# Mamba-2 scan and gated feed-forward on one core: the scan's visit for two pairs of sequences joined into one for all four, in chunks 2 to 5

## The chip, the core and the metric

The kernel runs on one core of a Trainium2 chip. Such a core has a matrix engine (TensorE, PE in the profile; its weight loads are PEld), an elementwise engine (VectorE, DVE), an activation engine (ScalarE, ACT), a general engine (GpSimd, POOL), and a queue for transfers (SyncE, SP). Each works through its own queue in order, and they wait for each other by semaphores. The metric is the device time of one execution in microseconds; lower is better.

## The reference

There are 4 sequences of 768 positions with 8 heads. Each head has a state of 16 by 32 (N by D). For chunks of positions, with L the product of the decays `a` between two positions:

```python
CB = np.einsum('bhin,bhjn->bhij', Cc, Bc)
y_intra = np.einsum('bhij,bhjd->bhid', CB * L, xc)
y_inter = np.einsum('bhin,bhnd->bhid', Cc, state) * decay_to_i[:, :, :, None]
y[:, :, sl] = y_intra + y_inter
Bx = np.einsum('bhjn,bhjd->bhjnd', Bc, xc) * decay_from_j[:, :, :, None, None]
state = decay_full[:, :, None, None] * state + np.sum(Bx, axis=2)
```

The heads' `y` side by side are the 256 columns of 3072 rows, which then go through a gated feed-forward layer in float32: `h = x @ w_in` (2048 columns), `g = h * cos(h)`, `out = g @ w_out`.

## The kernel before

**Chunks and steps.** The kernel takes chunks of 128 positions, so there are 6 of them, numbered 0 to 5, and in each all four sequences: 512 positions. The feed-forward part of one chunk is 16 steps, and a global step number `n` runs over all 96 (the loop at L739). `first(n)` makes one bank of `h` (hp, two banks in turn) by four matmuls with w_in; then ScalarE makes the whole turns `k`, VectorE the fraction `w` (L518), ScalarE the sine in place (L523, `gate`), and VectorE the product `gT` (L528, `gated`). Two steps later `second` multiplies it with w_out: from chunk 1 on by seven half-size products instead of eight (`seven`), for which GpSimd has to make differences `gd` of gT (L553 to L556) first. After steps 1 and 9 of a chunk's count, VectorE and ScalarE copy the finished banks to `ps`, GpSimd makes the output sums (L624), and SyncE stores them.

**The scan between the steps.** In chunks 1 to 5 the scan of one pair of sequences (`u` is 0 or 1; `b` is a sequence, two to a pair) is done in stages placed between the steps:

- `decays`: VectorE's running products `lam` (L344), two halves of four heads for each sequence, and GpSimd's scaled B, `sc`;
- `reaches` (L335): the running products of `a` along a chunk, one for each sequence;
- `turn2`: TensorE transposes B and C (tp), ScalarE copies them out as bT and cT, VectorE makes rT, which is C times the reach;
- `intra2`: TensorE's products C times B in two double banks, `g`;
- `masked`: VectorE's products `m` of g and lam, one sequence at a time;
- `finish2`, here called the visit: TensorE's products of the state (L447), then the products of m with x (L454), both into y; ScalarE copies y to yT, which is the input of the feed-forward part of that chunk; then the sums of the chunk (L471, `sum_up`), and `carry`, in which VectorE (`whole`) and GpSimd make the new state.

Two of the three products use only a strip of TensorE's 128 rows or columns, so four run beside each other: L447 on strips of 32 rows and 64 columns, L454 and L471 on 128 rows and 32 columns.

**The order.** The order of the queues is the order in which the program is written; no scheduler changes it. `TURN = (NF - 5, NF + 3)` with NF = 16 says at which step, counted from the start of the chunk before, a pair has its `turn2`: pair 0 at step 11, pair 1 at step 19, that is, step 3 of its own chunk. Its `intra2` is one step later, its `masked` one and two later, its visit three later, and its four half scans are at the four steps before it (chunk 1, pair 0, has its own places). So a visit comes every 8 steps, and half scans come one a step at most. In a step, VectorE's queue has w, rT if there is one, gT, the masked products, the carry, the half scan and then the reach scans. TensorE has first, the transposes, second, g and then the visit.

**Buffers.** tp, g, y and the sums take turns on two pairs of PSUM banks (`pair`), so y's bank is the first bank of g, and is free when masked has read it. `m` has two buffers in SBUF, rT, bT and cT one. `unit0`, `a0s` and `tos` are used at the start only and have memory of their own.

Of the kernel before, what the change touches and what calls it, by code (L numbers as in the profile page):

```python
# [8 lines left out]
FP32 = mybir.dt.float32  # L9
# [16 lines left out]
def kernel(  # L26
# [30 lines left out]
    V, ACT, G, PE = nc.vector, nc.scalar, nc.gpsimd, nc.tensor  # L57

    NB, H, S, D = x.shape
    N = B.shape[-1]  # L60
    P = 128
    NC = S // P
    DM, DF = moe_w_in.shape
    KT = DM // P
    NF = DF // P
    TB = NB * P
# [4 lines left out]
    W = P // 2  # L71

    const = ctx.enter_context(tc.tile_pool(name="const", bufs=1))
    loads = ctx.enter_context(tc.tile_pool(name="loads", bufs=3))
    rows = ctx.enter_context(tc.tile_pool(name="rows", bufs=NB))
    scan = ctx.enter_context(tc.tile_pool(name="scan", bufs=2))
# [3 lines left out]
    two = ctx.enter_context(tc.tile_pool(name="two", bufs=2))  # L80
# [8 lines left out]
    def pair(name):  # L89

        return psum.tile([P, 2, 4 * P], FP32, tag="scan", bufs=2, name=name)


    raw, arow, along = {}, {}, {}
# [124 lines left out]
    for b in range(NB):  # L219
# [4 lines left out]
        out=a_in, in_=a.rearrange("(u b) h (c p) -> (b h c) u p", u=NU, p=P))  # L224
# [9 lines left out]
    unit = const.tile([P, HH, P], FP32, name="unit")  # L234
    G.tensor_copy(out=unit, in_=ident.unsqueeze(1).to_broadcast([P, HH, P]))

    unit0 = const.tile([P, H, W], FP32, name="unit0")
    for t in range(2):
        ts = slice(t * W, (t + 1) * W)
        V.tensor_copy(out=unit0[ts], in_=ident[ts, ts].unsqueeze(1).to_broadcast([W, H, W]))  # L240
# [30 lines left out]
                    axis=mybir.AxisListType.XY, op=ALU.add)  # L271


    a0s = const.tile([P, 2, H, W], FP32, name="a0s")
    halves = a0z.rearrange("p (t i) -> p t i", t=2)
    for h in range(HH):
        ACT.activation(a0s[:, :, h], halves, AF.Copy, scale=mine[:, h:h + 1])
    for t in range(2):
        G.tensor_tensor(out=a0s[:, t, HH:H], in0=halves[:, t:t + 1].to_broadcast([P, HH, W]),
                        in1=mine[:, HH:H].unsqueeze(2).to_broadcast([P, HH, W]), op=ALU.mult)  # L280
    tos = const.tile([P, H, W], FP32, name="tos")
    G.tensor_tensor(out=tos, in0=to.unsqueeze(1).to_broadcast([P, H, W]),
                    in1=mine.unsqueeze(2).to_broadcast([P, H, W]), op=ALU.mult)

# [1 line left out]
    scaled, lam, reach, state, part, yT = {}, {}, {}, {}, {}, {}  # L286

    def heads(b):
        return slice(b * H, (b + 1) * H)
# [78 lines left out]
    def intra(b):  # L368
        bT, cT = part[0, b]
        g = [pair("g") for _ in range(2)]  # L370
        for q in range(4):
            r = slice(32 * q, 32 * q + 32)
            PE.matmul(g[q // 2][:, q % 2, 0:2 * P], lhsT=bT[r],
                      rhs=cT[r].rearrange("p t (s i) -> p s t i", s=2), start=True, stop=True)
        l = lam.pop((0, b))
        m = scan.tile([P, 2, H, W], FP32, tag="m", name="m")
        for q in range(2):
            of = [t[:, :, q * HH:(q + 1) * HH].rearrange("p s (k t) i -> p k s (t i)", k=2)
                  for t in (m, l)]
            V.tensor_tensor(out=of[0], in0=g[q][:, :, 0:2 * P].rearrange(  # L380
                "p k (s i) -> p k s i", s=2), in1=of[1], op=ALU.mult)
        part[0, b] = m
# [16 lines left out]
    def turn2(c, u):  # L399
        bc = raw[c][0]  # L400

        tp = pair("tp")[:, 0].rearrange("p (s k i) -> p s k i", s=2, k=2)
        for s in range(2):
            for k in range(2):
                PE.transpose(tp[:, s, k],  # L405
                             bc[:, k, heads(2 * u + s)].rearrange("p h n -> p (h n)"), ident)
        bT = scan.tile([P, 2, P], FP32, tag="bT2", bufs=1, name="bT2")
        ACT.copy(out=bT, in_=tp[:, :, 0])
        cT = scan.tile([P, 2, 2, P], FP32, tag="cT2", bufs=1, name="cT2")
        for t in range(2):  # L410
            ACT.activation(cT[:, :, t], tp[:, :, 1], AF.Copy, scale=slot[:, t:t + 1])
        rT = scan.tile([P, 2, P], FP32, tag="rT", bufs=1, name="rT")
        V.tensor_tensor(out=rT, in0=tp[:, :, 1], in1=reach[c, u], op=ALU.mult)
        part[c, u] = [bT, cT, rT]

# [10 lines left out]
    def masked(c, b):  # L426

        u, s = divmod(b, 2)
        g, ms = part[c, u][0:2]
        l = lam.pop((c, b))  # L430
        m = scan.tile([P, H, P], FP32, tag="m", name="m")
        for q in range(2):
            of = [t[:, q * HH:(q + 1) * HH].rearrange("p (k t) i -> p k (t i)", k=2)
                  for t in (m, l)]
            V.tensor_tensor(out=of[0], in0=g[q][:, :, s * 2 * P:(s + 1) * 2 * P], in1=of[1],  # L435
                            op=ALU.mult)
        ms.append(m)

    def finish2(c, u):
        (_, ms, rT), xr = part.pop((c, u)), raw[c][1]  # L440
        y = pair("y")


        for s in range(2):
            for q in range(4):
                r, p = slice(32 * q, 32 * q + 32), 64 * (q % 2)
                PE.matmul(y[p:p + 64, q // 2, s * P:(s + 1) * P],  # L447
                          lhsT=state[c - 1, u][r, s].rearrange("p t d -> p (t d)"),
                          rhs=rT[r, s], start=(s == 0), stop=False, tile_position=(32 * q, p),
                          skip_group_check=True)  # L450
        for s in range(2):
            for h in range(H):
                q, t = h % 4, h // 4
                PE.matmul(y[32 * q:32 * q + 32, t, s * P:(s + 1) * P], lhsT=xr[:, 2 * u + s, h],  # L454
                          rhs=ms[s][:, h], start=False, stop=True, tile_position=(0, 32 * q),
                          skip_group_check=True)
        if u == 0:
            yT[c] = two.tile([P, 2, TB], FP32, tag="yT", name="yT")
        ACT.copy(out=yT[c][:, :, 2 * u * P:(2 * u + 2) * P], in_=y[:, :, 0:2 * P])
        if c < NC - 1:  # L460
            s_ps = pair("s_ps")[:, 0, 0:4 * D].rearrange("p (s d) -> p s d", s=2)
            for s in range(2):
                sum_up(c, 2 * u + s, s_ps[:, s])
            carry(c, u, s_ps)

    def sum_up(c, b, s_ps):

        xr, sc = raw[c][1], scaled.pop((c, b))
        for q in range(4):
            two_ = slice(2 * q, 2 * q + 2)  # L470
            PE.matmul(s_ps[32 * q:32 * q + 32], lhsT=sc[:, two_].rearrange("p h n -> p (h n)"),  # L471
                      rhs=xr[:, b, two_].rearrange("p h d -> p (h d)"), start=True, stop=True,
                      tile_position=(0, 32 * q), skip_group_check=True)
# [47 lines left out]
    def gate(n):  # L521
        cos = turns[n]
        ACT.activation(cos, cos, AF.Sin, bias=quarter, scale=TWO_PI)  # L523
# [160 lines left out]
    for dst, src in ((a_cut, cut), (a_all, la)):  # L684
        nc.sync.dma_start(
            out=dst.rearrange("(u b) h (c p) -> (b h c) u p", u=NU, p=P), in_=src)
# [11 lines left out]
                 NF + 1: [(0, hind), (1, hind)], NF + 3: [(2, hind), (3, hind)]}  # L698


    TURN = (NF - 5, NF + 3)

    halves_of = {u: [(t - 4 + i, 2 * u + i // 2, i % 2) for i in range(4)]
                 for u, t in enumerate(TURN)}
    ahead = {1: {0: [(4, 0, 0), (6, 0, 1), (8, 1, 0), (9, 1, 1)]}}

    sums = {}

# [18 lines left out]

    def pairs(n):

        at = [(1 + (n - t) // NF, u) for u, t in enumerate(TURN) if (n - t) % NF == 0]  # L730
        return [(c, u) for c, u in at if 0 < c < NC]

    def halves_at(n):
        return [(c, b, t) for c in range(1, NC) for u in range(2)
                for m, b, t in ahead.get(c, {}).get(u, halves_of[u]) if m + (c - 1) * NF == n]

    EARLY = 3
    rest_of_loads()
    for n in range(NC * NF + LAG):  # L739
        c, f = divmod(n, NF)  # L740
        early = n < EARLY
        if n < NC * NF:
            if f == 0 and c > 0:
                load(c + 2)
            first(n)
            if n == 0:
                first_scan()
            for at in pairs(n):
                turn2(*at)
            rests = [grade(*piece[m], later=True)  # L750
                     for m in ((n,) if early else ()) + ((n + 1,) if n >= EARLY - 1 else ())
                     if m in piece]
            gate(n)
            for rest in rests:
                if rest:
                    rest()
            if not early and n in piece:
                join(*piece[n])
            gated(n)
            if early and n in piece:  # L760
                join(*piece[n])
            if n in (1, 2):
                carry(0, n - 1, sums[n - 1])
        for i, js in differ_at.get(n, ()):
            differ_w(i, js)
        if n >= LAG:
            second(n - LAG)
        for c, u in pairs(n - 1):
            intra2(c, u)
            masked(c, 2 * u)  # L770
        for c, u in pairs(n - 2):
            masked(c, 2 * u + 1)
        for c, u in pairs(n - 3):
            finish2(c, u)
            if u == 1:
                raw.pop(c)
        for c, b, t in halves_at(n):
            decays(c, b, t)
            if t == 1:
                load_a(c + 1, (b,))  # L780
        for c, u in pairs(n + 1):
            for b in (2 * u, 2 * u + 1):
                reaches(c, b)
                load_along(c + 1, (b,))
# [30 lines left out]
```

## Time and profile before

| | |
|---|---|
| time, median of 3 | 387.14 us (386.27 to 387.29) |
| profiled execution | 386.67 us, span 384.9 us |
| TensorE clock granted | 1.00 |
| L512, hp matmuls | 768, 184.4 us busy |
| L609, output products | 1106 in four forms, 274 to 277 ns each |
| L422 g, L454 y, L447 y, L471 sums | 160, 320, 160, 160 records |
| L344 lam | 40 scans, 1394 ns mean |
| L335 reach | 20 scans, 786 ns mean |
| L435 m | 40 products, 681 ns mean |

A float32 matmul stands as two records. The durations of matmuls overlap, as they are pipelined: what one costs is read from the distance between two starts (eight records of L512 take 1.73 us), not from its duration. Idle time of an engine is given with what ended it, in brackets.

### The profile page before, as it was taken

What the parts mean: (1) busy time and instruction counts of PE and PEld (TensorE: products, weight loads), DVE (VectorE), ACT (ScalarE), POOL (GpSimd) and SP (SyncE); (2) the same over time, 40 slices, a digit from 0 to 9 for tenths busy, and PEclk for the clock granted to TensorE, in tenths of its full rate; (3) what the DMA queues carried; (4) which work ended last, traced back from release to release, by engine and by line L of the source; (5) the groups of instructions that cost most, each with busy time, mean ns of one, the idle gap of its engine ahead of it and who ended that gap; (6) DMA issues with size and microseconds to landing.
All of it is one profiled execution on the core that took longest, in us unless ns stands there. A gap on an engine that the chain in (4) does not pass through costs nothing.

```text
span 384.9 us, 7726 instructions
## 1 busy us (share of the span) xinstructions
PE 378.3 (98%) x2982; PEld 331.2 (86%) x2982; DVE 265.9 (69%) x395; ACT 172.9 (45%) x303; POOL 245.4 (64%) x366
## 2 busy tenths in 40 slices
PE   8999999999999999999999999999999999999996
PEld 3578887888899899899899899899899989989995
DVE  7879999678667658657657757756765865863443
ACT  3878566534334334335334434434433433433441
POOL 5757665458859549648648837855955855853751
PEclk9999999999999999999999999999999999999999
DMA  7989899975002951301791301201210000010001
GB/s 83 270 235 266 249 230 137 181 96 151 2 0 63 148 52 57 96 2 54 127 81 55 97 2 56 81 17 43 68 43 1 21 10 0 2 27 3 7 22 27
DMA packets 106371, 30.42 MB, mean 79 GB/s; under 512 B 75520, under 2 KB 102240, under 8 KB 106336
## 3 DMA queue, kind: packets, MB, share of 16 engines
q1 hardware_dynamic: 106176, 29.81, 38.9%
q8 instruction: 23, 0.38, 0.5%
q10 hardware_dynamic: 160, 0.13, 0.1%
q14 instruction: 12, 0.10, 0.1%
HBM read 26.59 MB, written 3.34 MB: 78 GB/s over the span
## 4 chain that ended last, share of the span: by engine, by line
PE 82%; DVE 7%; POOL 3%; ACT 2%; issue 2%; DMA 2%; SPq 1%; ACTq 0%
PE hp L512 37%; PE o L609 32%; PE g L422 3%; PE y L454 3%; DVE mag L209 2%; DVE w L518 2%; DMA xr<-in_x_dram 2%; PE y L447 2%; DVE lam L344 2%; PE o L571 1%; DVE gT L528 1%; PE warm L101 1%; ACT w L523 1%; PE a_ps L298 1%; PE tp L405 1%
## 5 line engine op out<-in xcount | busy, mean ns | idle before, releaser
L512 PE MATMUL hp<-yT,w_in 128*128 128x256 f32 x768 | 184.4, 383 | 0.6 <-POOL w_in L217 0.3
L512 PEld LDWEIGHTS hp<-yT,w_in 128*128 128x128 f32 x768 | 139.2, 190 | 22.7 <-issue 4.5
L553 POOL TENSOR_TENSOR gd<-gT 128x256 f32<-128x256 f32 x79 | 71.9, 911 | 89.5 <-DVE gT L528 86.2
L528 DVE TENSOR_TENSOR gT<-hp,w 128x512 f32<-128x512 f32 x96 | 66.3, 691 | 69.9 <-ACT w L523 60.1
L523 ACT ACTIVATE w<-w,quarter 128x512 f32<-128x512 f32 x96 | 69.3, 722 | 97.2 <-DVE w L518 97.2
L516 ACT ACTIVATE k<-hp 128x512 int32<-128x512 f32 x96 | 57.1, 595 | 90.8 <-PE hp L512 90.7
L518 DVE SCALAR_TENSOR_TENSOR w<-hp,k 128x512 f32<-128x512 f32 x96 | 65.4, 681 | 36.7 <-ACT k L516 36.4
L609 PE MATMUL o<-words,gd 128*128 128x128 f32 x474 | 67.0, 277 | 0.6 <-POOL gd L555 0.6
L609 PEld LDWEIGHTS o<-words,gd 128*128 128x128 f32 x474 | 59.3, 192 | 2.4 <-POOL gd L555 2.2
L344 DVE TENSOR_TENSOR_SCAN lam<-arow,unit 128x512 f32<-128x512 f32 x40 | 55.7, 1394 | 0.0
L609 PEld LDWEIGHTS o<-w_out,gT 128*128 128x128 f32 x316 | 46.9, 191 | 3.6
L609 PE MATMUL o<-w_out,gT 128*128 128x128 f32 x316 | 48.0, 274 | 0.0
L555 POOL TENSOR_TENSOR gd<-gT,gd 128x128 f32<-128x128 f32 x79 | 43.1, 546 | 6.2
L556 POOL TENSOR_TENSOR gd<-gT,gd 128x128 f32<-128x128 f32 x79 | 35.9, 455 | 6.2
L571 PE MATMUL o<-w_out,gT 128*128 128x256 f32 x128 | 30.3, 380 | 0.4 <-POOL w_out L217 0.4
L609 PE MATMUL o<-w_out,gd 128*128 128x128 f32 x158 | 30.6, 275 | 0.0
L609 PE MATMUL o<-words,gT 128*128 128x128 f32 x158 | 30.5, 275 | 0.0
L571 PEld LDWEIGHTS o<-w_out,gT 128*128 128x128 f32 x128 | 24.2, 190 | 4.0 <-POOL w_out L217 0.8
L435 DVE TENSOR_TENSOR m<-g,lam 128x512 f32<-128x512 f32 x40 | 25.6, 681 | 0.0
L624 POOL TENSOR_TENSOR sum<-ps,sum 128x256 f32<-128x256 f32 (+1 forms) x27 | 24.2, 909 | 1.4
L609 PEld LDWEIGHTS o<-w_out,gd 128*128 128x128 f32 x158 | 24.0, 192 | 0.0
L609 PEld LDWEIGHTS o<-words,gT 128*128 128x128 f32 x158 | 24.0, 192 | 0.0
(91 smaller groups left out, 293.9 us busy)
## 6 DMA issues: line engine op xcount, KB each, us to landing
arow<-a_cut SPq DMA_DIRECT2D x20, 512.0 KB
words<-in_moe_w_in_dram SPq DMA_DIRECT2D x8, 512.0 KB
words<-in_moe_w_out_dram SPq DMA_DIRECT2D x8, 512.0 KB
out_dram<-sum SPq DMA_DIRECT2D x18, 128.0 KB
xr<-in_x_dram SPq DMA_DIRECT2D x4, 512.0 KB
along<-a_all SPq DMA_DIRECT2D x20, 64.0 KB
xr<-in_x_dram SPq DMA_DIRECT2D x8, 128.0 KB
bc<-in_B_dram SPq DMA_DIRECT2D x4, 256.0 KB
```

Source lines behind the costliest of these rows:

```text
L344: V.tensor_tensor_scan(out=lam[c, b][:, hs].rearrange("p h i -> p (h i)"), data0=rows_.rearrange("p h i -> p (h i)"), data1=unit.rearrange ...
L435: V.tensor_tensor(out=of[0], in0=g[q][:, :, s * 2 * P:(s + 1) * 2 * P], in1=of[1], op=ALU.mult)
L512: PE.matmul(to_[:, e], lhsT=w_in[:, k, fs], rhs=y[:, k, u], start=(k == 0), stop=(k == KT - 1), skip_group_check=True)
L516: ACT.activation(k, hp[n], AF.Copy, bias=0.25, scale=INV_2PI)
L518: V.scalar_tensor_tensor(out=w, in0=hp[n], scalar=INV_2PI, in1=k, op0=ALU.mult, op1=ALU.subtract)
L523: ACT.activation(cos, cos, AF.Sin, bias=quarter, scale=TWO_PI)
L528: V.tensor_tensor(out=gT[n], in0=hp.pop(n), in1=cos, op=ALU.mult)
L553: G.tensor_tensor(out=d[:, 0:2], in0=g[:, 1:2].to_broadcast([P, 2, P]), in1=g[:, 3::-3], op=ALU.subtract)
L555: G.tensor_tensor(out=d[:, 2], in0=g[:, 0], in1=d[:, 0], op=ALU.subtract)
L556: G.tensor_tensor(out=d[:, 3], in0=g[:, 2], in1=d[:, 2], op=ALU.subtract)
L571: PE.matmul(o[c, u][:, t], lhsT=g[:, 2 * e + t], rhs=w_out[:, 2 * j + e], start=(j == e == t == 0), stop=(j == NJ - 1 and e == 1), skip_gr ...
L609: PE.matmul(at[q], lhsT=a_[q], rhs=w[q], start=(j == 0 and q in starts), stop=(j == NJ - 1), skip_group_check=True)
```

## The change

For chunks 2 to 5 the visits of the two pairs are joined: one `finish2` does the state's products of all four sequences, then all y products, then all sums, and the two carries. The two stages of transposes and g stay apart, and both come ahead of it: at steps 6 and 10 of the chunk before, and the visit at step 13. Thus all of a chunk's y stands before its feed-forward steps begin. The aim is that TensorE changes between its whole array and the strips half as often. Chunk 1 keeps two visits, the second one step earlier. A list `plan` now says for every chunk which pairs, at which steps the transposes and half scans are, and when the visit is. For this, m gets four buffers and rT two; the room comes from unit0, tos and a0s, which now live in buffers of m.

```diff
-    unit0 = const.tile([P, H, W], FP32, name="unit0")
+    both = scan.tile([P, 2, H, W], FP32, tag="m", bufs=4, name="both")
+    unit0, tos = both[:, 0], both[:, 1]
...
-    a0s = const.tile([P, 2, H, W], FP32, name="a0s")
+    a0s = scan.tile([P, 2, H, W], FP32, tag="m", bufs=4, name="a0s")
...
-        rT = scan.tile([P, 2, P], FP32, tag="rT", bufs=1, name="rT")
+        rT = scan.tile([P, 2, P], FP32, tag="rT", name="rT")
...
-        m = scan.tile([P, H, P], FP32, tag="m", name="m")
+        m = scan.tile([P, H, P], FP32, tag="m", bufs=4, name="m")
...
-    def finish2(c, u):
-        (_, ms, rT), xr = part.pop((c, u)), raw[c][1]
+    def finish2(c, us):
+
+        xr = raw[c][1]
+        parts = [(2 * u + s, part[c, u][1][s], part[c, u][2][:, s]) for u in us for s in range(2)]
         y = pair("y")
-        for s in range(2):
+        for i, (b, _, rT) in enumerate(parts):
             for q in range(4):
                 r, p = slice(32 * q, 32 * q + 32), 64 * (q % 2)
-                PE.matmul(y[p:p + 64, q // 2, s * P:(s + 1) * P],
-                          lhsT=state[c - 1, u][r, s].rearrange("p t d -> p (t d)"),
-                          rhs=rT[r, s], start=(s == 0), stop=False, tile_position=(32 * q, p),
+                PE.matmul(y[p:p + 64, q // 2, i * P:(i + 1) * P],
+                          lhsT=state[c - 1, b // 2][r, b % 2].rearrange("p t d -> p (t d)"),
+                          rhs=rT[r], start=(i == 0), stop=False, tile_position=(32 * q, p),
                           skip_group_check=True)
-        for s in range(2):
+        for i, (b, m, _) in enumerate(parts):
...
-        if c < NC - 1:
-            s_ps = pair("s_ps")[:, 0, 0:4 * D].rearrange("p (s d) -> p s d", s=2)
-            for s in range(2):
-                sum_up(c, 2 * u + s, s_ps[:, s])
-            carry(c, u, s_ps)
+        if c < NC - 1:
+            for u in us:
+                carry(c, u, s_ps[:, u, :, 0:2 * D])
...
-    TURN = (NF - 5, NF + 3)
-
-    halves_of = {u: [(t - 4 + i, 2 * u + i // 2, i % 2) for i in range(4)]
-                 for u, t in enumerate(TURN)}
-    ahead = {1: {0: [(4, 0, 0), (6, 0, 1), (8, 1, 0), (9, 1, 1)]}}
+    late = [((0,), {0: 11}, [(4, 0, 0), (6, 0, 1), (8, 1, 0), (9, 1, 1)], 14),
+            ((1,), {1: NF + 2}, [(NF - 2 + i, 2 + i // 2, i % 2) for i in range(4)], NF + 5)]
+    whole_ = [((0, 1), {0: 6, 1: 10}, [(2, 0, 0), (3, 0, 1), (5, 1, 0), (5, 1, 1),
+                                       (6, 2, 0), (7, 2, 1), (9, 3, 0), (10, 3, 1)], 13)]
+    plan = [(c, NF * (c - 1), *v) for c in range(1, NC) for v in (late if c == 1 else whole_)]
...
-        for c, u in pairs(n - 3):
-            finish2(c, u)
-            if u == 1:
+        for c, us in ends(n):
+            finish2(c, us)
+            if 1 in us:
                 raw.pop(c)
```

In `plan`, an entry has the pairs of the visit, the step of each pair's transposes, the half scans as (step, sequence, half), and the step of the visit, all counted from the start of the chunk before.

More of the change, by code (lines that the diff above doesn't have):

```diff
@@ L280 @@
                         in1=mine[:, HH:H].unsqueeze(2).to_broadcast([P, HH, W]), op=ALU.mult)
-    tos = const.tile([P, H, W], FP32, name="tos")
     G.tensor_tensor(out=tos, in0=to.unsqueeze(1).to_broadcast([P, H, W]),
@@ L375, in intra @@
         l = lam.pop((0, b))
-        m = scan.tile([P, 2, H, W], FP32, tag="m", name="m")
+        m = scan.tile([P, 2, H, W], FP32, tag="m", bufs=4, name="m")
         for q in range(2):
@@ L450, in finish2 @@
                           skip_group_check=True)
-        for s in range(2):
+        for i, (b, m, _) in enumerate(parts):
             for h in range(H):
                 q, t = h % 4, h // 4
-                PE.matmul(y[32 * q:32 * q + 32, t, s * P:(s + 1) * P], lhsT=xr[:, 2 * u + s, h],
-                          rhs=ms[s][:, h], start=False, stop=True, tile_position=(0, 32 * q),
+                PE.matmul(y[32 * q:32 * q + 32, t, i * P:(i + 1) * P], lhsT=xr[:, b, h],
+                          rhs=m[:, h], start=False, stop=True, tile_position=(0, 32 * q),
@@ L456, in finish2 @@
                           skip_group_check=True)
-        if u == 0:
-            yT[c] = two.tile([P, 2, TB], FP32, tag="yT", name="yT")
-        ACT.copy(out=yT[c][:, :, 2 * u * P:(2 * u + 2) * P], in_=y[:, :, 0:2 * P])
+        s_ps = pair("s_ps")[:, 0].rearrange("p (u s d) -> p u s d", u=2, s=2)
+        for i, u in enumerate(us):
+            del part[c, u]
+            if u == 0:
+                yT[c] = two.tile([P, 2, TB], FP32, tag="yT", name="yT")
+            ACT.copy(out=yT[c][:, :, 2 * u * P:(2 * u + 2) * P],
+                     in_=y[:, :, 2 * i * P:(2 * i + 2) * P])
+            for s in range(2 if c < NC - 1 else 0):
+                sum_up(c, 2 * u + s, s_ps[:, u, s, 0:2 * D])
@@ L728, in pairs, with ends @@
     def pairs(n):
-        at = [(1 + (n - t) // NF, u) for u, t in enumerate(TURN) if (n - t) % NF == 0]
-        return [(c, u) for c, u in at if 0 < c < NC]
+        return [(c, u) for c, at, _, turn_at, _, _ in plan for u in turn_at
+                if at + turn_at[u] == n]
     def halves_at(n):
-        return [(c, b, t) for c in range(1, NC) for u in range(2)
-                for m, b, t in ahead.get(c, {}).get(u, halves_of[u]) if m + (c - 1) * NF == n]
+        return [(c, *h) for c, at, _, _, halves_of, _ in plan for m, *h in halves_of if at + m == n]
+    def ends(n):
+        return [(c, us) for c, at, us, _, _, end in plan if at + end == n]
     EARLY = 3
```

## The prediction

> **What bounds the kernel now.** I read the page's busy table first, then the chain of work that ended last:
>
> ```profile
> PE 378.3 (98%) x2982; PEld 331.2 (86%) x2982; DVE 265.9 (69%) x395; ACT 172.9 (45%) x303; POOL 245.4 (64%) x366
> PE 82%; DVE 7%; POOL 3%; ACT 2%; issue 2%; DMA 2%; SPq 1%; ACTq 0%
> ```
>
> TensorE sets the time: 98% busy, 82% of the chain. A change gains only by taking time off TensorE's queue, and loses whenever TensorE waits for another engine. Next the TensorE timeline of one visit of the scan in chunk 3, between two steps of the feed-forward part:
>
> ```profile
> 133.69 0.39 PE L609 MATMUL o<-w_out,gd 128*128 128x128 f32 x2
> 134.00 0.67 PE L447 MATMUL y<-rT,state 32*64 32x128 f32 x16
> 134.60 1.08 PE L454 MATMUL y<-m,xr 128*32 128x128 f32 x32
> 135.50 0.41 PE L471 MATMUL s_ps<-xr,sc 128*32 128x64 f32 x16
> 135.83 1.99 PE L512 MATMUL hp<-yT,w_in 128*128 128x256 f32 x8
> ```
>
> Then eight steps (half a chunk), cut at each first hp matmul, to see how long a step is and how busy the others are. Columns: stretch, us, then busy of PE, PEld, DVE, ACT, POOL. The rows are a plain step, one with transposes (`tp`), one with `g`, and one with the visit:
>
> ```profile
> 145.80:149.09 3.29, 3.29 (x24) 3.08 (x23) 2.43 (x4) 1.69 (x3) 2.77 (x5) 1.00 0.54 159
> 149.09:152.82 3.73, 3.73 (x28) 3.47 (x27) 2.87 (x5) 2.33 (x5) 3.50 (x5) 1.00 0.02 4
> 152.82:157.53 4.71, 4.71 (x41) 3.86 (x39) 3.41 (x6) 1.93 (x3) 4.16 (x8) 1.00 0.40 104
> 160.92:166.13 5.21, 5.21 (x88) 4.62 (x86) 3.20 (x6) 2.12 (x4) 1.79 (x4) 1.00 0.00 0
> ```
>
> Last, VectorE and GpSimd around it, for the engine that could make TensorE wait:
>
> ```profile
> 147.29 0.68 DVE L619 COPY ps<-o 128x512 f32<-128x512 f32 x1
> 147.89 1.44 DVE L344 TENSOR_TENSOR_SCAN lam<-arow,unit 128x512 f32<-128x512 f32 x1
> 149.25 0.66 DVE L518 SCALAR_TENSOR_TENSOR w<-hp,k 128x512 f32<-128x512 f32 x1
> 150.77 0.69 DVE L528 TENSOR_TENSOR gT<-hp,w 128x512 f32<-128x512 f32 x1 [0.86 <-ACT w L523]
> 151.38 1.31 DVE L344 TENSOR_TENSOR_SCAN lam<-arow,unit 128x512 f32<-128x512 f32 x1
> 152.61 1.42 DVE L335 TENSOR_TENSOR_SCAN reach<-along,ones 128x128 f32<-128x128 f32 x2
> 153.95 0.66 DVE L518 SCALAR_TENSOR_TENSOR w<-hp,k 128x512 f32<-128x512 f32 x1
> ...
> 148.32 1.25 POOL L555 TENSOR_TENSOR gd<-gT,gd 128x128 f32<-128x128 f32 x1
> ```
>
> VectorE is 69% busy, but between `w` and `gT` its queue stands 0.86 us for ScalarE's sine. From the start of `w` to the slot after `gT` takes 2.16 (141.84 to 144.00); one `lam` scan takes 1.13 (144.00 to 145.13). Together 3.29: with one scan a step VectorE just keeps TensorE's pace. The slack that 69% suggests is not there.
>
> **What the Trainium skill says.** "TensorEngine Tiling", Key Properties: changing the tiling mode drains TensorE. The trace agrees: inside the y products groups of four records start every 0.109 us, while from the last state group to the first y group 0.218 pass, and the first hp matmul follows the last group of sums by 0.16, where sums come every 0.056. "TensorE: Matmul & The Clock Gate", Part 1: ScalarE and VectorE are strict FIFO; the 0.86 us agree. "SBUF — State Buffer", Who interferes with whom: a VectorE instruction with two SBUF inputs and a GpSimd one that reads SBUF block each other. It agrees: `gd` L555, mean 0.55, takes 1.25 beside a `lam` scan, and the scan 1.44, against a least of 1.21.
>
> **The change, part by part.**
>
> *One visit for two, chunks 2 to 5.* A visit costs 5.21 − 3.29 = 1.92, and 0.10 in the step after (160.92 − 157.53 = 3.39 after `g`, and the same after a visit): 2.02. A joined visit adds the second pair's streaming alone: 4 groups of state products and 8 of y at 0.109, 4 of sums at 0.056, 0.44 + 0.87 + 0.22 = 1.53. So it costs 3.55 for 4.04: saved 0.49 a chunk, about 1.9 us for four (the last chunk has no sums, with much the same drains). Transposes (0.44) and `g` keep their number.
>
> *Carry.* Four `whole` for two, at 0.28 each, with one wait for GpSimd as `whole` has one buffer. In a visit step VectorE now idles 2.11 us before `w`, which hides it: nothing. The second `yT` copy on ScalarE (0.59) lies there too.
>
> *Buffers.* Four m buffers, with a0s, unit0 and tos moved in, and two of rT: the instructions at the start keep their order and waits. Nothing.
>
> *Chunk 1.* Its second visit comes a step earlier, and chunk 2's scans begin at step 18, while GpSimd still makes the weights' differences. Before, TensorE loses 0.75 us there to `gd` (one wait in chunk 1). I take this as equal; it may grow by 1 us.
>
> *The scan's VectorE work, moved together.* The eight half scans, spread before over 16 steps at one a step, now stand at steps 2, 3, 5, 5, 6, 7, 9, 10 of the chunk before, the reach scans at 5 and 9, masks at 7, 8, 11, 12. I follow the lag L: how much later `w` starts than 2.62 us after its step's first matmul (141.84 − 139.22). L grows by VectorE's work less the step's length. Checked on the lines above: the step at 142.51 with copy and scan (2.16 + 0.60 + 1.36 − 3.29) gives 0.83, and `w` is at 149.25 = 145.80 + 2.62 + 0.83. The next, scan 1.24 and two reaches 1.34, gives 2.25; measured 153.95 − 151.71 = 2.24.
>
> The new order is priced at both ends. Undisturbed: scan 1.13, reach pair 0.62 (its shortest row is 0.39). Beside GpSimd: at step 9, which has the output sums as the lines above have, scan 1.36 and pair 1.34; at step 5 the three `gd` (0.73, 0.45, 0.45 alone) slip in between, and I let the first hold the second scan up by 0.47 (1.60) and the others the reaches by 0.33 (0.95), an estimate. A mask pair is 1.20 (132.10 to 133.30). Step lengths: 3.29, with tp 3.73, with g 4.46 (4.71 less a 0.25 wait for `gd`: 1.81 for 1.56 in the chain), 3.39 after g.
>
> - Step 5, two scans and reaches: L = 1.75 to 2.55 at step 6.
> - Step 6, one scan: 1.28 to 2.08. Step 7, mask and scan: 1.31 to 2.11 at step 8.
> - Step 8: `gT` ends 4.86 + L after the step began, and hp has two banks, so the matmuls two steps on wait for it; a wait of this kind shows 0.14 from end to start (60.38 to 60.52). TensorE arrives after 3.39 + 3.29 = 6.68, `gT` allows 6.31 to 7.11: wait 0 to 0.4. With the mask, L is 1.28 to 2.08 at step 9.
> - Step 9, copy, scan, reaches: L at step 10 is 2.5 to 3.8. TensorE reaches step 12's hp 8.19 after step 10 began, allowed at 7.5 to 8.8: wait 0 to 0.6.
> - Steps 11 and 12: L falls to 0.9 to 1.7; the last mask, whose bank y takes, is ready 6.5 to 7.3 after step 12 began, TensorE is there at 6.8: wait 0 to 0.5.
>
> Queued behind `w` and `gT` are the sine, GpSimd's three `gd` and then TensorE's second product of that step; the `gd` waits of now, 0.25 in each half chunk, I carry over unchanged: the sums at steps 1 and 9 still meet scans.
>
> So waits of 0 to 1.5 a chunk. I take 1.0, nearer the upper end: in this trace every scan beside a GpSimd operation was lengthened or lengthened the other, and at steps 5 and 9 four and three scans stand in a row beside GpSimd work. Sum: (1.0 − 0.49) × 4 = 2.0: 387.1 + 2.0 = 389.1, say 389.0.
>
> **The rivals.**
>
> *The waits vanish.* With scans at the low prices hp is always free in time, and 387.1 − 1.9 = 385.2 remains. For it: TensorE's own waits lengthen steps and let VectorE catch up, and steps 0, 1, 4, 14 and 15 have no scan. If the sums at step 1, now with less VectorE work beside them, also lose their 0.25, it is 384.2. Against it: the lag of 2.24 that one scan and one pair make already.
>
> *They cancel:* waits of about 0.5 a chunk, 387.1. It needs chance more than a mechanism.
>
> *The lag feeds itself.* Late `gT` makes `gd` late, `gd` meets the next scan and the output sums, and TensorE waits twice, 2.5 a chunk: 387.1 + 4 × 2.0 = 395. For it: GpSimd is at 4.16 of 4.71 in the step with g. Against: 4 empty steps clear any backlog each chunk.
>
> *Loads late.* arow of the next chunk is issued as its buffer's scan ends, so still a chunk ahead; the DMA share is under 0.6 there. I give it no chance of its own.
>
> **How the numbers follow.** Forecast, waits of 0.7 to 1.9 a chunk: 0.47. Vanish: 0.35. Cancel: 0.13. Feeds itself: 0.05. So slower 0.52, same 0.13, faster 0.35. The range takes the vanishing waits down to 384.5 and waits of 1.7 a chunk up to 392.0; about 0.1 is left out above and 0.08 below.
>
> **What would show it.** Right: y in 32, 64 and 32 records at one place a chunk, 3.5 us long, in chunks 2 to 5; `w` 2 to 2.6 us late at step 6 and over 3 at step 10; new idle of hp before step 10 or 12 released by `gT`, and a little before y released by m. Wrong: if hp and y show no such idle, the time falls to 385; if transposes to g or the joined visit cost more than 3.6, the saving was over-rated; if idle of the second product released by `gd` grows above 0.5 a chunk, the part that I carried over was mis-sized, and chunk 1's end is the next place to look.

## The result and the profile after

The changed kernel takes 389.46 us (median, 388.95 to 389.69) against 387.07 for the kernel before on the same chip: a ratio of 1.0064 with an interval of 1.0046 to 1.0081. It is slower, by 2.4 us. The span of the profiled execution goes from 384.9 to 387.9 us at a granted clock of 1.00; 0.3 of these 3.0 us lie ahead of the first `hp`, whose start lies between 17.9 and 19.1 us in the traces of this case.

The same two lines of the page as in the prediction, busy time and the chain of work that ended last, now of the kernel after:

```profile
PE 377.6 (97%) x2982; PEld 331.1 (85%) x2982; DVE 265.4 (68%) x395; ACT 171.7 (44%) x303; POOL 246.3 (64%) x366
PE 59%; DVE 25%; ACT 7%; issue 4%; POOL 3%; DVEq 0%; ACTq 0%; POOLq 0%
```

The busy line hardly shows the loss: every engine does what it did. The chain does. TensorE's share falls from 82% to 59% and VectorE's rises from 7% to 25%: in long stretches the end now hangs on VectorE's queue. So the question is where TensorE waits for it. For that the trace is cut at each first `hp` matmul, and the length of each step is compared with that of its kind before.

**What the change was for came.** The TensorE timeline of the joined visit in step 13 of chunk 2, where chunk 3's scan stands (by this count the visit that the prediction shows is in step 14 of chunk 1 and is chunk 2's, not chunk 3's). Columns are start, duration, engine, line:

```profile
195.37 1.10 PE L450 MATMUL y<-rT,state 32*64 32x128 f32 x32
196.40 1.95 PE L457 MATMUL y<-m,xr 128*32 128x128 f32 x64
198.18 0.63 PE L478 MATMUL s_ps<-xr,sc 128*32 128x64 f32 x32
198.74 0.70 PE L519 MATMUL hp<-yT,w_in 128*128 128x256 f32 x2
```

From 195.37 to 198.74 TensorE does not stop. The step as a whole takes 6.75 (its window stands below), 3.46 more than a plain one of 3.29, and 0.10 more fall in the next: 3.56 for what was 4.04. For the scan of chunk 5, which has no sums, it is 3.11 for 3.60. The four joined visits together save 1.93 us.

**The waits that took its place.** Windows of the kernel after: step 9, step 10, step 12 and step 13 of chunk 2. As in the prediction, the stretch and its length, then busy time and number of instructions of PE, PEld, DVE, ACT and POOL; the last three numbers are the granted clock, the DMA share and GB/s.

```profile
175.35:179.29 3.94, 3.45 (x24) 3.08 (x23) 3.08 (x5) 1.21 (x2) 2.13 (x4) 1.00 0.31 92
179.29:184.14 4.85, 4.33 (x27) 3.65 (x27) 3.99 (x6) 2.59 (x6) 3.08 (x5) 1.00 0.13 37
188.60:191.99 3.39, 3.39 (x27) 3.18 (x23) 2.53 (x5) 1.32 (x2) 3.15 (x7) 1.00 0.35 82
191.99:198.74 6.75, 6.75 (x153) 6.16 (x151) 3.88 (x7) 2.36 (x4) 3.41 (x7) 1.00 1.02 152
```

Steps 12 and 13 have PE busy for their whole length. On TensorE, step 9 has nothing but hp and the second product; it should take 3.29 and takes 3.94. Step 10 has transposes; it should take 3.73 and takes 4.85. In both, PE is busy for less than the stretch. What ended the idle time stands on the TensorE timeline of the second of them, in brackets:

```profile
179.29 1.97 PE L519 MATMUL hp<-yT,w_in 128*128 128x256 f32 x8 [0.49 <-DVE gT L535]
181.09 0.60 PE L406 MATMUL tp<-ident,bc 128*128 128x128 f32 x4
182.12 0.71 PE L616 MATMUL o<-w_out,gT 128*128 128x128 f32 x4 [0.42 <-ACT ps L625]
182.66 1.19 PE L616 MATMUL o<-words,gd 128*128 128x128 f32 x6
```

There are two waits. The first is one that the prediction named: hp of step 10 stands for `gT` of step 8, as hp has two banks. Its bracket says 0.49, the step is 0.65 longer. The bracket counts from the end of the last record (178.80), and in an unbroken step the next hp starts 0.16 before that end (178.64, which is 175.35 + 3.29): 0.49 + 0.16. The second wait the prediction did not name. The second product of step 10 starts a new pair of output banks. Those were filled up to step 9, and must first be copied out by ScalarE (L625, three blocks) and VectorE (L626, four blocks). Both copies are issued after step 9's gate and `gT`, and these are late. ScalarE and VectorE at that place:

```profile
180.97 0.72 ACT L530 ACTIVATE w<-w,quarter 128x512 f32<-128x512 f32 x1 [2.14 <-DVE w L525]
181.60 0.46 ACT L625 COPY ps<-o 128x384 f32<-128x384 f32 x1
```

```profile
165.25 2.82 DVE L345 TENSOR_TENSOR_SCAN lam<-arow,unit 128x512 f32<-128x512 f32 x2
168.00 1.14 DVE L336 TENSOR_TENSOR_SCAN reach<-along,ones 128x128 f32<-128x128 f32 x2
169.06 0.66 DVE L525 SCALAR_TENSOR_TENSOR w<-hp,k 128x512 f32<-128x512 f32 x1
...
178.45 0.69 DVE L535 TENSOR_TENSOR gT<-hp,w 128x512 f32<-128x512 f32 x1 [0.86 <-ACT w L530]
...
182.41 0.68 DVE L626 COPY ps<-o 128x512 f32<-128x512 f32 x1
```

ScalarE idles 2.14 us for a late `w`, runs the sine, and only then the copy that TensorE's queue is standing for; VectorE's own copy ends at 183.09, so the other bank comes still later, within the group of six at 182.66 (its third record needs it, and starts at 183.14). Where the lateness starts is at the top of the VectorE lines: two scans in a row at step 5 take 2.75 us (165.25 to 168.00), the two reaches 1.06, all ahead of step 6's `w`.

The whole account, by steps (a wait is the length of a step less its length when nothing is waited for):

| where | before | after |
|---|---|---|
| chunk 1: step 4 before, step 5 after | 0.82 (gd) | 0.80 (y for m) |
| steps 9 and 10 of chunk 1 (the scan is chunk 2's) | | 0.26 + 1.12 |
| steps 9 of chunks 2 to 4 (hp for gT) | | 3 × 0.65 |
| steps 10 of chunks 2 to 4 (output banks for copies) | | 3 × 1.11 |
| `gd`, steps with g or sums | 8 × about 0.26, and 0.28 | 3 × 0.11 |
| sum | 3.16 | 7.79 |

7.79 − 3.16 − 1.93 saved = +2.70; the traces differ by 2.70 from step 8 of chunk 0 to the end, the times by 2.4. Nothing large is missing from the account.

### The profile page after: what moved, and what is told of

It is laid out like the page before. It is cut to its first block, busy times and chain, and to the rows that moved or that the text cites. A ratio compares the mean times of both kernels' runs of the same rounds, so it can differ in the third digit from the quotient of the medians.

```text
span 387.9 us, 7704 instructions
## 1 busy us (share of the span) xinstructions
PE 377.6 (97%) x2982; PEld 331.1 (85%) x2982; DVE 265.4 (68%) x395; ACT 171.7 (44%) x303; POOL 246.3 (64%) x366
## 4 chain that ended last, share of the span: by engine, by line
PE 59%; DVE 25%; ACT 7%; issue 4%; POOL 3%; DVEq 0%; ACTq 0%; POOLq 0%
PE hp L519 27%; PE o L616 22%; DVE lam L345 8%; ACT w L530 5%; DVE w L525 5%; DVE gT L535 4%; DVE m L436 3%; PE y L457 2%; DVE mag L209 2%; PE g L423 1%; PE o L578 1%; PE y L450 1%; PE warm L101 1%; PE a_ps L299 1%; DVE reach L336 1%
## 5 line engine op out<-in xcount | busy, mean ns | idle before, releaser
L560 POOL TENSOR_TENSOR gd<-gT 128x256 f32<-128x256 f32 x79 | 63.9, 809 | 89.3 <-DVE gT L535 83.8
L345 DVE TENSOR_TENSOR_SCAN lam<-arow,unit 128x512 f32<-128x512 f32 x40 | 57.3, 1441 | 0.0
L563 POOL TENSOR_TENSOR gd<-gT,gd 128x128 f32<-128x128 f32 x79 | 43.3, 549 | 6.2
L562 POOL TENSOR_TENSOR gd<-gT,gd 128x128 f32<-128x128 f32 x79 | 43.3, 548 | 6.2
L631 POOL TENSOR_TENSOR sum<-ps,sum 128x256 f32<-128x256 f32 (+1 forms) x27 | 23.1, 869 | 1.4
```

Source lines behind the costliest of these rows:

```text
L345: V.tensor_tensor_scan(out=lam[c, b][:, hs].rearrange("p h i -> p (h i)"), data0=rows_.rearrange("p h i -> p (h i)"), data1=unit.rearrange ...
L560: G.tensor_tensor(out=d[:, 0:2], in0=g[:, 1:2].to_broadcast([P, 2, P]), in1=g[:, 3::-3], op=ALU.subtract)
L562: G.tensor_tensor(out=d[:, 2], in0=g[:, 0], in1=d[:, 0], op=ALU.subtract)
L563: G.tensor_tensor(out=d[:, 3], in0=g[:, 2], in1=d[:, 2], op=ALU.subtract)
```

## The experiments

The theory: VectorE's backlog, made by the scans that stand together (two at step 5 with the reaches, then one a step), makes gT and the output copies late, and TensorE waits for these two. The rivals: the waits belong to something that the change brought beside it (the long visit itself, GpSimd's `gd`, the bank hand-over) and stay when the scans are moved. Each diff is against the kernel after, where nothing else is said. Each ratio is to runs of the kernel before that were taken beside the experiment (their medians lie between 386.4 and 386.7 us), so experiments are best compared by their ratios.

**1. One scan a step earlier.** The second of the two scans of step 5 is all that is touched.

```diff
-    [(2, 0, 0), (3, 0, 1), (5, 1, 0), (5, 1, 1), (6, 2, 0), ...
+    [(2, 0, 0), (3, 0, 1), (4, 1, 0), (5, 1, 1), (6, 2, 0), ...
```

> One half scan (sequence 1, first half) is moved from step 5 to the empty step 4, in chunks 2 to 5. Theory A (VectorE's lag, begun by the two scans at step 5, makes TensorE wait at step 10 for hp and for the output banks): w at step 6 is 1.3 to 1.6 us late instead of 2.67, the 0.65 us before the hp of step 10 goes in chunks 3 to 5, the 1.11 us in step 10 shrinks to about 0.5; time 385.5 to 386.5. Theory B (GpSimd's port is the limit, so that the scan meets the output sums of step 1 at step 4 instead of gd at step 5): no gain, 389 to 390.

Measured: 385.98 us (385.24 to 386.35), 0.9977 of the kernel before (0.9966 to 0.9989), about 3.4 us less than after. `w` is 1.44 late at step 6 instead of 2.67, and 2.94 at step 10 instead of 3.51. Step 9 is 3.29: its wait is gone. Step 10 is 4.26, a wait of 0.53 left. On the weight loads of that step:

```profile
182.20 0.52 PEld L616 LDWEIGHTS o<-words,gd 128*128 128x128 f32 x4 [0.28 <-DVE ps L626]
```

What is left is VectorE's output copy. Step 4, which took the scan, is unchanged at 3.40. One scan a chunk, of 1.13 us on VectorE, moved by one step, takes away more than the whole change had cost. Chunk 2's scan is not helped: step 22 (step 6 of chunk 1) gets a wait of 0.35 that it did not have, where `w` of step 21 is now 3.58 late instead of 1.93. The theory's backlog holds; a cause that is independent of where the scan stands falls.

**2. The two visits apart again, all else as after.** Pair 0 at step 13, pair 1 at step 14.

```diff
-        return [(c, us) for c, at, us, _, _, end in plan if at + end == n]
+        return ([(c, us[:1]) for c, at, us, _, _, end in plan if at + end == n] +
+                [(c, us[1:]) for c, at, us, _, _, end in plan if at + end + 1 == n and len(us) > 1])
```

> The changed kernel with its places for scans, transposes and g, but the visit of chunks 2 to 5 cut in two again: pair 0 at step 13, pair 1 at step 14. It undoes the joining alone. If the joined visit saves four drains of 0.49 us, as worked out: 391.2 to 391.7, with every wait of the changed kernel unchanged. If joining saves nothing and only the places matter: 389.5.

Measured: 391.48 us (391.18 to 391.62), 1.0125 of before (1.011 to 1.0141), 2.0 us more than after by the times, 2.0 by the traces, 2.4 by the ratios. Steps 13 and 14 take 5.21 and 5.31 (5.21 is what such a step took before), every other wait stays. So joining is worth about 2.0 us in four chunks, 0.5 each, and the joined visit has no part in the waits.

**3. The output copies ahead of the gate.** In step 9 of chunks 1 to 4, the second product that ends the banks and its two copies are issued behind the step's `w` but before its sine and gT; GpSimd's sums stay where they were.

```diff
...
+            sums_later = (second(n - LAG, True) if n % NF == NJ + 1 and NF < n < NF * (NC - 1)
+                          else None)
             gate(n)
...
-        if n >= LAG:
+        if n < NC * NF and sums_later:
+            sums_later()
+        elif n >= LAG:
             second(n - LAG)
```

> At step 9 of chunks 1 to 4 the two copies of the output banks to ps are issued ahead of the sine and of gT, so that they don't stand behind VectorE's lag (VectorE waits for the sine there anyway). Theory A1 (the 1.11 us in step 10 is the wait for these copies): it goes, and w at step 10 is 0.6 earlier; the 0.65 before step 10's hp stays: 385 to 386. Theory A2 (lag is what matters, and a wait removed here comes back at the hp of steps 11 and 12 or at gd): 388 to 389.5.

Measured: 387.05 us (386.26 to 387.67), 1.0007 of before (0.9997 to 1.0016). TensorE in step 10, and two lines of VectorE, whose copy (L625 in this kernel) now lies ahead of gT:

```profile
177.62 1.97 PE L519 MATMUL hp<-yT,w_in 128*128 128x256 f32 x8 [0.49 <-DVE gT L535]
...
179.87 0.61 PE L615 MATMUL o<-w_out,gT 128*128 128x128 f32 x4
```

```profile
179.19 0.68 DVE L625 COPY ps<-o 128x512 f32<-128x512 f32 x1
180.14 0.69 DVE L535 TENSOR_TENSOR gT<-hp,w 128x512 f32<-128x512 f32 x1 [0.27 <-ACT w L530]
```

The o product has no bracket any more and step 10 is 3.80 instead of 4.84; the wait of hp, 0.49 in the bracket, stays as it was. So the wait at step 10 is the copies', and separate from the one at step 9. But of the 1.04 a chunk 0.48 come back: steps 12 and 13 are 0.39 and 0.09 longer. On the weight loads of step 12:

```profile
188.45 0.74 PEld L615 LDWEIGHTS o<-words,gd 128*128 128x128 f32 x6 [0.32 <-POOL gd L562]
```

The pause at step 10 had let VectorE catch up (`w` was 1.93 late at step 11; now 2.80). Without it the lag lives on and reaches TensorE two steps later by way of gT and `gd`. The result lies between what the two theories expected: the wait is the one named, and its removal is worth about half its size while the backlog stays.

**4. One scan more.** The half scan of step 7 is done twice for chunks 2 to 5 (work added that the result does not need).

```diff
         for c, b, t in halves_at(n):
             decays(c, b, t)
+            if c > 1 and (b, t) == (2, 1):
+                again(c, b, t)
```

> The half scan of step 7 is done twice (the same values again), in chunks 2 to 5: VectorE has 1.13 us more a chunk, TensorE and GpSimd nothing. Theory A (VectorE's lag): the wait before step 10's hp grows by about 1.1 us a chunk and the wait for the copies stays, 393.5 to 394.5. Theory B (GpSimd or the transfers set the waits): under 390.5.

Measured: 396.57 us (396.35 to 396.76), 1.0258 of before (1.0243 to 1.0273): some 7 us more than after, above what was expected. `w` at step 8 is 4.24 late, 1.88 more. A scan is only 1.13 of that. The rest is an effect of the edit (L357 is the repeated scan; the lines behind it are higher by 9):

```profile
178.53 1.22 DVE L357 TENSOR_TENSOR_SCAN lam<-arow,unit 128x512 f32<-128x512 f32 x1 [0.66 <-POOL sc L328]
```

The repeat overwrites a `lam` that GpSimd's `sc` is reading, and waits 0.66 for it. In the scan of chunk 5, which has no `sc`, the lag grows by 1.33. TensorE then stands long for hp of step 10, and afterwards is slow as well. Its lines at that place in chunk 1 and in chunk 2, and four windows of 2 us from the second:

```profile
118.71 1.97 PE L528 MATMUL hp<-yT,w_in 128*128 128x256 f32 x8 [1.89 <-DVE gT L544]
...
181.96 3.51 PE L528 MATMUL hp<-yT,w_in 128*128 128x256 f32 x8 [2.30 <-DVE gT L544]
```

```profile
180.00:182.00 2.00, 0.04 (x1) 0.07 (x1) 1.21 (x3) 1.21 (x2) 0.04 (x1) 1.00 0.44 135
182.00:184.00 2.00, 2.00 (x6) 1.59 (x7) 1.60 (x3) 0.36 (x1) 1.60 (x3) 0.55 0.42 127
184.00:186.00 2.00, 2.00 (x10) 1.63 (x9) 1.61 (x3) 1.16 (x3) 0.73 (x1) 0.59 0.00 0
186.00:188.00 2.00, 2.00 (x18) 1.95 (x17) 2.00 (x3) 1.20 (x4) 1.89 (x3) 1.00 0.04 8
```

The column to read is the third from the right, the granted clock: 0.55 and 0.59 in the 4 us after a pause of 2.30, then 1.00 again. Read more finely it is 0.50 from 182.21 to 185.62. Eight hp records take 3.51 instead of 1.97. A second pause of 2.30, in chunk 3, ends at 245.91, and the clock is 0.50 from 247.06 to 250.47; after the pauses of 1.89 in chunk 1 and of 1.82 in chunk 4 it stays at 1.00. So the run shows that VectorE's lag has no slack left to hide in (step 9's wait grows from 0.65 to 2.47), but its size mixes three things: the scan, the wait for `sc`, and the clock.

**5. Both mends.** Experiments 1 and 3 together.

> The edits of the first two runs together: the scan at step 4, and the copies ahead of the sine at step 9. If the two waits (0.65 before the hp of step 10, 1.11 for the copies) were the whole loss of chunks 3 to 5, both go: 383.5 to 385, and the step with gd at 12 shows at most 0.4. If the lag that is left only shifts the wait to hp of steps 11 to 12 or to gd, as with the copies alone: 385.5 to 386.5.

Measured: 383.34 us (382.94 to 383.68), 0.9927 of before (0.9912 to 0.9942). For the scans of chunks 3 to 5, step 9 is 3.29, step 10 is 3.73, step 12 is 3.39, and there is no wait but 0.11 at step 4. The prediction's rival in which the waits vanish gave 385.2, or 384.2 without the `gd` waits of step 1, from a base of 387.1; the ratio puts this run at 384.2 on that base. What remains is in chunk 1: 0.80, 0.36, 0.25 and 0.38 at steps 21, 22, 25 and 28, and under 0.1 at steps 26 and 29.

**6. The scans spread to where VectorE idles.** Experiment 5's copies, and for the scans of chunks 3 to 5 no step with two half scans, and none in the steps of the output copies (1 and 9) or of the masks 8 and 12: half scans at 0, 3, 4, 5, 6, 7, 10 and 11. The places of chunk 2's scan stay as after.

```diff
+    rest_ = [(*whole_[0][:2], [(0, 0, 0), (3, 0, 1), (4, 1, 0), (5, 1, 1),
+              (6, 2, 0), (7, 2, 1), (10, 3, 0), (11, 3, 1)], 13)]
...
```

> As the last, and the half scans of chunks 3 to 5 at steps 0, 3, 4, 5, 6, 7, 10, 11 (none beside the output sums of step 1, none in the steps of masks 8 and 12), chunk 2 as in the changed kernel. VectorE's lag at step 10 should fall to about 1.5, the 0.11 wait at step 4 and any gd wait at step 12 go: 383 to 384.3. If what is left of the waits is GpSimd's own work, not the lag: as the run before, within 0.3.

Measured: 383.06 us (382.6 to 383.21), 0.9918 of before (0.9901 to 0.9934). Its steps 9 and 10, to be laid beside those of the kernel after:

```profile
175.10:178.40 3.30, 3.30 (x24) 3.09 (x23) 2.44 (x5) 1.80 (x3) 1.49 (x4) 1.00 0.53 159
178.40:182.10 3.70, 3.70 (x27) 3.47 (x26) 3.44 (x7) 2.60 (x6) 2.00 (x5) 1.00 0.02 4
```

PE fills both. `w` is 0.98 late at step 10, where after had 3.51. In the trace, the steps with the scans of chunks 3 to 5 have no wait left; against experiment 5 the times do not tell the two apart, as that one had only 0.11 a chunk to lose. It is the best kernel found: by the ratios 3.2 us faster than before, and 5.6 faster than after (experiment 9), with the same number of instructions on every engine. What is left is in chunk 1: steps 25 and 28 are still 0.25 and 0.38 too long, and there is one wait of TensorE that has a bracket between 80 and 330 us, at step 21:

```profile
100.31 0.67 PE L450 MATMUL y<-rT,state 32*64 32x128 f32 x16 [0.74 <-DVE m L436]
```

**7. The early copies in the kernel before.** A control: is experiment 3's edit good in itself? The diff is the same, on the kernel before.

> The kernel before, with the copies of step 9 ahead of the sine and of gT, as a control. There VectorE is not late at step 9, so that no wait for the copies is to be taken away: no gain, 386.3 to 387.5, perhaps slower as the copies now hold up the sine. If early copies pay of themselves (shorter hold of the output banks, earlier sums): over 0.5 us faster.

Measured: 386.02 us (385.08 to 386.63), 0.9987 of before (0.9978 to 0.9995): a small gain, about 0.5 us, where none or a loss was expected. The steps with g of pair 0 are 4.56 instead of 4.71. The copy's 0.6 leaves VectorE's lag ahead of that step (0 at step 10 instead of 0.83), so gT and `gd` come earlier. The copies do not bind the kernel before; of the 3.2 us of experiment 6 about 0.5 could be had from this edit without the joined visit.

**8. Chunk 1's second visit one step later.** Experiment 6 with the visit at step 22, against the wait of y for m shown above. The diff is against experiment 6.

```diff
-            ((1,), {1: NF + 2}, [(NF - 2 + i, 2 + i // 2, i % 2) for i in range(4)], NF + 5)]
+            ((1,), {1: NF + 2}, [(NF - 2 + i, 2 + i // 2, i % 2) for i in range(4)], NF + 6)]
```

> As the run with the scans spread, and chunk 1's second visit at step 22, where it is in the kernel before, instead of 21. If the 0.73 us before y at step 21 is the last mask standing behind VectorE's lag of 2 us there: it goes, 382.2 to 382.6, unless the scans of chunk 2, which then come before the carry, push w at step 22 later. If it only moves into step 22 or 23: as the run before, within 0.3.

Measured: 385.90 us (383.55 to 386.74), 0.9984 of before (0.9973 to 0.9995): a miss, slower than experiment 6. The wait of y is gone, but TensorE's visit now stops inside:

```profile
107.22 0.63 PE L478 MATMUL s_ps<-xr,sc 128*32 128x64 f32 x16 [2.39 <-DVE rT L414]
107.78 3.43 PE L519 MATMUL hp<-yT,w_in 128*128 128x256 f32 x8
```

```profile
102.37 2.82 DVE L345 TENSOR_TENSOR_SCAN lam<-arow,unit 128x512 f32<-128x512 f32 x2
105.11 1.14 DVE L336 TENSOR_TENSOR_SCAN reach<-along,ones 128x128 f32<-128x128 f32 x2
...
106.76 0.41 DVE L414 TENSOR_TENSOR rT<-tp,reach 128x256 f32<-128x256 f32 x1
```

The visit at step 22 meets the transposes of chunk 2, whose `turn2` is at the same step: the sums' bank is the pair that tp uses, and tp is let go by rT, which stands behind two scans, two reaches and a `w` on VectorE. After 2.39 us of idle the clock falls to half here as well (0.50 from 107.31 to 110.72, hp 3.43 us). That is most of the loss: 17 of the 18 runs have a mean granted clock of 0.995 or 0.996 and take 385.1 to 386.7 us; the one with 1.000 takes 383.55, hardly more than experiment 6. So the later visit trades a wait of 0.74 for one of 2.39 that mostly takes the clock down as well, and the change was right to bring it to step 21.

**9. The kernel after once more**, unedited, on the chip of experiment 8.

> The changed kernel unedited on the same chip as the run beside it, to have the experiments' differences on one base: 0.6 percent over the kernel before.

Measured: 389.39 us (388.76 to 389.69), 1.0062 of before (1.0045 to 1.0078): the result repeats.

## Why the prediction was right, and where not

The forecast was 389.0, slower by 1.9; measured were 389.46 and 2.4. The mechanism was right: VectorE's backlog makes TensorE wait, and joining saves what was worked out. That the sum came out so near is in part luck, because two misses have opposite signs. By its steps:

- **One visit for two**: 3.55 for 4.04 was worked out from spacings; the trace has 3.56, and experiment 2 gives 2.0 us for four. Right.
- **Carry, buffers**: no new wait shows for either. Right.
- **Chunk 1 equal**: 0.75 before was taken over; in steps it is 0.82 before and 0.80 after. Right in size, but not in cause: the wait for `gd` went, and one of y for m came with the visit a step earlier.
- **The lag**: the ranges and what was measured, in us (the prediction gives no figure for step 11):

| `w` late at step | 6 | 7 | 8 | 9 | 10 | 11 | 12 |
|---|---|---|---|---|---|---|---|
| predicted | 1.75–2.55 | 1.28–2.08 | 1.31–2.11 | 1.28–2.08 | 2.5–3.8 | – | 0.9–1.7 |
| measured | 2.67 | 2.20 | 2.36 | 2.29 | 3.51 | 1.93 | 0.80 |

The course of the lag is there: 0.1 to 0.25 above the range at steps 6 to 9, inside it at step 10, and just below it at step 12, after TensorE's waits in steps 9 and 10. The terms behind it: the upper price of two scans in a row was 1.13 + 1.60 and 2.75 was measured; the reaches beside `gd` were put at 0.95 and took 1.06. The GpSimd product that overlaps both scans is this one. Alone it takes 0.73:

```profile
165.48 1.51 POOL L560 TENSOR_TENSOR gd<-gT 128x256 f32<-128x256 f32 x1 [1.50 <-DVE gT L535]
```

The upper price rested on the Trainium skill, "SBUF — State Buffer", Who interferes with whom, and the trace agrees: two scans that take 2.26 alone took 2.75, and the product 1.51 for 0.73. At step 5 the lag follows the upper price; at step 9 the reaches took 1.06, where 1.34 was that price, and the lag stays 0.3 under the upper end.

- **Waits of hp before step 10**, 0 to 0.4: it came, 0.65 in chunks 2 to 4. Right in cause and too small, because the lag at step 8 was 0.25 above the range: with the measured 2.36, the prediction's own sum gives 4.86 + 2.36 + 0.14 − 6.68 = 0.68. The 0.14 from the end of `gT` to hp holds: 179.14 to 179.29.
- **Waits before step 12 and before y**, 0 to 0.6 and 0 to 0.5: neither came in chunks 2 to 5. TensorE's new pauses in steps 9 and 10 let VectorE catch up first; the prediction had followed the lag with step 10 at its undisturbed length of 3.73.
- **What failed** is in "Queued behind `w` and `gT` are the sine, GpSimd's three `gd` and then TensorE's second product": the output copies of step 9 are queued there too, on both engines, and new output banks stand for them. This wait, 1.11 a chunk, is the largest of all, and experiment 3 shows it by taking it away. It could have been read before. In the VectorE lines that the prediction shows, the copy of 147.29 ends at 147.97. TensorE at that place, in the kernel before:

```profile
147.53 0.61 PE L609 MATMUL o<-w_out,gT 128*128 128x128 f32 x4
147.98 0.83 PE L609 MATMUL o<-words,gd 128*128 128x128 f32 x6
```

The first four records and the first two of the six write ScalarE's bank; the third of the six, at 148.20, is the first for VectorE's. So the margin was 0.23, against a lag that the prediction itself put at 1.3 to 2.1. By its own method the wait can be worked out: that record starts 2.40 after its step began (145.80), with transposes 2.84; in the kernel after the copy ends 3.80 after step 10 began, 0.96 too late, of the 1.11 measured.
- **The `gd` waits "carried over unchanged"**: they were 0.50 a chunk before and 0.11 after. The steps with g now stand at 7 and 11 instead of 4 and 12; whether it is their distance from the output sums of steps 1 and 9 that matters, no run here separates. This is the miss on the other side.

Per chunk: waits 0.65 + 1.11 − 0.39 = 1.37 where 1.0 was taken, less 0.48 saved, is +0.89 where the forecast had +0.51. Of these 1.37 the wait that the forecast did not name is by far the largest; where experiment 3 takes it away, the kernel is no longer clearly slower than before (1.0007). So the forecast had the right cause and the right sign, but a good part of its 1.0 stood for waits that did not come, in place of one that did. The rival in which the waits vanish was no fancy: experiments 5 and 6 are that kernel, and two of its conditions were a scan's place and a copy's.

## What to carry to other kernels

When work is gathered in one place to save on the engine that sets the time, ask what the gathering does to the engines that feed it: here it saved 1.9 us on TensorE, but put VectorE 2 to 3.5 us behind in the middle of each chunk, with over 30% of VectorE's time unused elsewhere. Follow a backlog step by step and list everything that stands in the late queue, copies that free a bank included; the margin of each such hand-over can be read in the kernel before. Removing one wait gives back only part of it as long as the backlog remains (0.56 of 1.04 in experiment 3); spread the work first.

## What the hardware showed that was not expected

- A pause of TensorE can cost more than itself. After 2.30 us of idle (twice in experiment 4) and 2.39 (experiment 8) the granted clock is 0.50 for 3.4 us, and this begins 0.1 to 1.2 us after TensorE has started again. After pauses of 1.89 and 1.82 in the same run of experiment 4, and of 0.42 to 0.73 in the kernel after, it stays at 1.00. In the traces the limit thus lies between 1.89 and 2.30, but the length of the pause is not all that counts: of the 18 runs of experiment 8, one kept a mean clock of 1.000. "TensorE: Matmul & The Clock Gate", Part 1, in the Trainium skill, puts the fall back to half rate after an idle window of about 3.4 us; here 2.30 us were enough.
- A short pause is longer than its bracket: 0.49 in the bracket, 0.65 in the length of the step, as records of TensorE overlap by 0.16 where it does not pause.
- Scans and GpSimd products that overlap lengthen each other: the pair of scans, 2 × 1.13 alone, took 2.75, while GpSimd's two products beside it took 1.51 and 1.25 instead of 0.73 and 0.46.
